# Attention and MoE on one core: the last batch's attention moved behind the start of the first pair, the sums of w_in moved to step 38, and a planner that prices VectorE and GpSimd meeting on a port

## The chip, the cores and the metric

One core of one Trainium2 chip runs the whole program. The metric is device time in microseconds; three runs of the kernel before took 879.83, 882.25 and 883.19 us, median 882.25. Engines are named as in the profile: PE is TensorE, DVE is VectorE, ACT is ScalarE, POOL is GpSimd, and SP is the queue from which nearly all DMAs are issued.

## The reference

Eight batches of softmax attention in its linear form (keys' softmax over the sequence, queries' over the head's 64 columns) feed a feed-forward block with a squared ReLU. All is float32.

```python
q_s = softmax(q, axis=-1); k_s = softmax(k, axis=2)      # 8 batches, 8 heads, 576 rows, 64 columns
kv = np.einsum('bhsd,bhse->bhde', k_s, v)
attn_out = np.einsum('bhsd,bhde->bhse', q_s, kv)
x = attn_out.transpose(0, 2, 1, 3).reshape(B * S, H * D)  # 4608 x 512
r = np.maximum(x @ w_in, 0.0)                             # w_in 512 x 2048
out = (s * (r * r) + b) @ w_out                           # w_out 2048 x 512
```

## The kernel before

**Blocks and steps.** Each batch gives one block of 512 rows; the 64 rows left over of each batch together form a ninth block. The 2048 inner columns are cut into 16 chunks. Blocks 0 to 4 run as 80 steps (`step(t)`, block t // 16, chunk t % 16): 12 matmuls make `h` for a chunk, ACT and DVE turn it into `r` and then into a high and a low float32r half (`gh`, `gl`; L1148, L1161, L1163, L1165), and 12 matmuls add it into the block's outputs (`acc`). Each product of two float32 numbers is three matmuls of such halves.

**Pairs.** Blocks 5 and 6, and then 7 and 8, run as pairs. For a pair, the first layer is done by a seven-product scheme instead of eight: `product` (L918) multiplies sums of quarters of w_in (names A11, S1 to S4 in `PROD`, stored in DRAM as `aset`, brought back through a ring of eight buffers by `ring_loads`) by sums of quarters of the two blocks (`B..`, `T..`), which lie as halves in the old weight slots (`b_cast`, `b_sums`, `stage_loads`). The sums of w_in's quarters are made on POOL by `a_sums`: 16 jobs of seven POOL instructions (L801, L804, four of L808, L812), one cast on ACT and two stores each. `quadrant` turns the products of one of eight rounds into four chunks; two of them go on at once, two are spilt to DRAM and come back later.

**Attention.** The attention of batches 2 to 7 goes on beside the steps. A batch has two `pr` (8 to 15 here are called pr 4 to 15, two per batch), each with two head pairs `u` (8 to 31). For a `pr`, `k_late` finds the keys' column maxima on DVE, sends them through DRAM (`k_out` L533, `k_in` L537), subtracts them and `k_exps` takes the exponential; `q_late` does the queries with two POOL instructions (L597, L614), and sends the turned halves through DRAM (L627, L634); `kv_late` and `x_late` make the matmuls on PE and evict them. Batches 3 and 4 write their result to DRAM and `x_back` brings it back in 512 KB pieces (L761), which ACT and DVE split into halves (L764, L766). In the kernel before all of it, but for the end of the last batch, stands ahead of the first pair.

**What sets the order.** `Order.run` is a planner that runs while the program is built. Every piece of work is a stream of `Op`s with an engine, a cost, a due time, needs (names of other ops' results, with a margin `late`) and buffers taken and freed; the planner takes the op that can start first (within NEAR the one due first), so that each engine's queue has a fixed order. At run time each engine then takes its queue in that order and an instruction waits for its data; everything behind it on that engine or queue waits too. The needs and costs exist in the planner alone: they change the order, not what an instruction waits for.

## Time and profile before

| what | value |
|---|---|
| median of three runs | 882.25 us |
| profiled execution | 883.05 us |
| its span, first to last instruction | 881.3 us |
| mean granted PE clock | 0.993 |
| PE busy | 844.0 us, 96% |
| DVE busy | 591.6 us, 67% |
| ACT busy | 440.2 us, 50% |
| POOL busy | 201.1 us, 23% |

The profiled execution lies 0.8 us above the median, and 1.75 us of it lie around its span. Busy shares are means over stages that differ: steps up to about 547 us, the first pair from there, the second pair from about 708 us. A wait is written with the engine that ended it; a line's idle time is that of its engine just before it.

### The profile page before, as it was taken

How to read it: one execution, taken by the hardware profiler on the slowest of the kernel's cores; microseconds unless marked ns; L12 is line 12 of the kernel's file. 1: busy time of each engine (PE TensorE's matmuls, PEld its weight loads, DVE VectorE, ACT ScalarE, POOL GpSimd, SP SyncE). 2: the span in 40 equal slices, each digit the busy share in tenths (PEclk: the TensorE clock that was granted, in tenths of full speed). 3: DMA queues.
4: the chain of work that ended last, by engine and by line, in shares of the span. 5: the costliest groups of instructions: out<-in, count | busy, mean ns of one | idle time of the engine just before them, and what ended most of it. 6: DMA issues, size and time to landing. Idle time of an engine off the chain costs nothing.

```text
span 881.3 us, 12571 instructions
## 1 busy us (share of the span) xinstructions
PE 844.0 (96%) x4358; PEld 690.6 (78%) x4358; DVE 591.6 (67%) x940; ACT 440.2 (50%) x720; POOL 201.1 (23%) x233
## 2 busy tenths in 40 slices
PE   7999999988999889987999999999999999999998
PEld 6788887877777668776788878888888888888886
DVE  6999977989987787867889764544457234434430
ACT  5998644644453454534455766533346243333430
POOL 1000035745662462435322232000013000000000
PEclk9999999999999999998999999999999999999999
DMA  9999157776679666767887734885554346555421
GB/s 274 322 387 304 58 150 204 200 189 160 185 184 241 172 178 183 204 183 193 201 232 182 184 101 118 276 265 153 165 152 161 85 143 193 157 161 159 167 73 48
DMA packets 175828, 161.82 MB, mean 184 GB/s; under 512 B 56468, under 2 KB 143508, under 8 KB 175764
## 3 DMA queue, kind: packets, MB, share of 16 engines
q1 hardware_dynamic: 174612, 159.89, 64.4%
q10 hardware_dynamic: 1152, 1.11, 0.4%
q8 instruction: 35, 0.57, 0.3%
q14 instruction: 29, 0.24, 0.1%
HBM read 106.43 MB, written 54.54 MB: 183 GB/s over the span
## 4 chain that ended last, share of the span: by engine, by line
PE 65%; DVE 16%; DMA 8%; issue 4%; ACT 3%; POOL 2%; SPq 1%; ACTq 0%; DVEq 0%; POOLq 0%
PE acc L1186 27%; PE h L1123 12%; PE bankU L932 10%; PE bankV L932 7%; PE last L1102 5%; DVE r L1161 2%; DMA back<-xs 2%; DVE gl L1165 2%; DMA area<-in_q_dram 2%; DVE y L722 2%; DMA turned<-area 1%; DVE area L623 1%; PE kv L314 1%; DVE area L618 1%; DVE kvf L672 1%
## 5 line engine op out<-in xcount | busy, mean ns | idle before, releaser
L1186 PE MATMUL acc<-w,gh 128*128 128x512 f32 x1024 | 319.5, 393 | 0.0
L1123 PE MATMUL h<-x,w 128*128 128x512 f32 x960 | 238.3, 395 | 9.8 <-ACT r L1148 9.7
L1186 PEld LDWEIGHTS acc<-w,gh 128*128 128x128 f32 x1024 | 190.3, 188 | 38.8 <-ACT o L1203 0.4
L1123 PEld LDWEIGHTS h<-x,w 128*128 128x128 f32 x960 | 180.4, 190 | 49.8 <-ACT r L1148 11.7
L1186 PE MATMUL acc<-w,gl 128*128 128x512 f32 x512 | 201.6, 394 | 4.7 <-DVE gl L1165 4.6
L1186 PEld LDWEIGHTS acc<-w,gl 128*128 128x128 f32 x512 | 96.4, 188 | 28.8 <-DVE gl L1165 8.4
L932 PE MATMUL bankU<-w,ring 128*128 128x512 f32 x378 | 96.0, 390 | 0.0
L1148 ACT ACTIVATE r<-h 128x512 f32<-128x512 f32 x80 | 47.7, 596 | 75.0 <-PE h L1123 64.1
L932 PEld LDWEIGHTS bankU<-w,ring 128*128 128x128 f32 x378 | 70.9, 188 | 14.6
L1009 DVE TENSOR_TENSOR rows<-bankV,rows 128x512 f32<-128x512 f32 x48 | 33.2, 691 | 61.1 <-PE bankV L932 31.4
L1163 ACT ACTIVATE gh<-r,sb 128x512 fp32r<-128x512 f32 x69 | 49.8, 722 | 44.3 <-DVE r L1161 43.8
L932 PE MATMUL bankV<-w,ring 128*128 128x512 f32 x282 | 71.6, 389 | 0.0
L1017 DVE SCALAR_TENSOR_TENSOR rows<-rows,sb 128x512 f32<-128x512 f32 x64 | 49.2, 772 | 32.6 <-ACT rows L1011 23.5
L1165 DVE SCALAR_TENSOR_TENSOR gl<-r,sb,gh 128x512 fp32r<-128x512 f32 x69 | 62.7, 909 | 7.1 <-ACT gh L1163 6.3
L1161 DVE SCALAR_TENSOR_TENSOR r<-r,sb 128x512 f32<-128x512 f32 x69 | 57.7, 836 | 14.6 <-ACT r L1148 14.4
L932 PEld LDWEIGHTS bankV<-w,ring 128*128 128x128 f32 x282 | 53.0, 188 | 11.0
L597 POOL TENSOR_TENSOR area<-area,qm 128x640 f32<-128x640 f32 x24 | 32.9, 1372 | 88.4 <-DVE qm L595 76.1
L904 POOL TENSOR_TENSOR stage<-stage 128x1024 f32<-128x1024 f32 x8 | 21.4, 2675 | 138.4 <-DVE w L889 138.1
L1011 ACT ACTIVATE rows<-rows 128x512 f32<-128x512 f32 x48 | 30.1, 627 | 43.9 <-DVE rows L1009 43.9
L1007 ACT COPY rows<-bankU 128x512 f32<-128x512 f32 x48 | 28.2, 588 | 47.2 <-PE bankU L932 47.1
L1029 DVE SCALAR_TENSOR_TENSOR gl<-rows,sb,gh 128x512 fp32r<-128x512 f32 x32 | 24.0, 751 | 35.8 <-ACT gh L1027 35.7
L614 POOL TENSOR_TENSOR qe<-qe,qr 128x640 f32<-128x640 f32 x24 | 33.5, 1396 | 43.7 <-DVE qr L610 16.0
(159 smaller groups left out, 1056.1 us busy)
## 6 DMA issues: line engine op xcount, KB each, us to landing
ring<-aset SPq DMA_DIRECT2D x110, 256.0 KB, 2.9
spare<-turned SPq DMA_DIRECT2D x48, 320.0 KB, 6.0
st<-in_moe_w_in_dram SPq DMA_DIRECT2D x16, 512.0 KB, 7.6
st<-in_moe_w_out_dram SPq DMA_DIRECT2D x16, 512.0 KB, 8.4
out_dram<-o SPq DMA_DIRECT2D x16, 512.0 KB, 3.1
aset<-S SPq DMA_DIRECT2D x32, 256.0 KB, 3.4
spilt<-rows SPq DMA_DIRECT2D x32, 256.0 KB, 3.1
turned<-qe SPq DMA_DIRECT2D x24, 320.0 KB, 3.5
```

The source lines that it names most:

```text
L597: nc.gpsimd.tensor_tensor(out=qt, in0=qt, in1=bc(qm, [P, 2, NT, D]), op=ALU.subtract)
L614: nc.gpsimd.tensor_tensor(out=qe_, in0=qe_, in1=qr, op=ALU.mult)
L932: nc.tensor.matmul(out_, w[:, a, c * P:(c + 1) * P], slot(k, c)[:, b_], start=k in (0, 1, 3) and n == 0, stop=n == 5, skip_group_check=True)
L1009: nc.vector.tensor_tensor(out=row(), in0=BANK["V"], in1=row(), op=ALU.add)
L1017: nc.vector.scalar_tensor_tensor(out=r, in0=r, scalar=s_col, in1=r, op0=ALU.mult, op1=ALU.mult)
L1102: nc.tensor.matmul(banks[j], g[:, js], w_, start=(f == 0 and n == 0), stop=(f == NFC - 1 and n == 2))
L1123: nc.tensor.matmul(hp_, w[:, j, c, :], x[:, c, :], start=(c == 0 and i == 0), stop=(c == NP - 1 and i == 2))
L1148: nc.scalar.activation(r, hp_, AF.Relu)
L1161: nc.vector.scalar_tensor_tensor(out=r, in0=r, scalar=s_col, in1=r, op0=ALU.mult, op1=ALU.mult)
L1163: nc.scalar.activation(gh, r, AF.Identity, bias=b_col)
L1165: nc.vector.scalar_tensor_tensor(out=gl, in0=r, scalar=b_col, in1=gh.bitcast(F32), op0=ALU.add, op1=ALU.subtract)
L1186: nc.tensor.matmul(acc[blk, j // 2][:, j % 2], g[:, js], w_, start=(f == 0 and i == 0), stop=(f == NFC - 1 and i == 2))
```

## The change

The planner's `Op` gets a kind "DVEp" for DVE instructions that read two tensors from SBUF: where POOL is planned busy at their start, 0.65 of the meeting is added to their cost. `k_fold` is priced 0.7 instead of 0.5. `WAIT`, the margin ahead of attention's matmuls, goes from 1.5 to 2.5. `a_sums` may not be planned before the step of its due time, and these run from step 38 at 2.4 steps each instead of from 18 at 3.5. The last batch's loads (pr 14 and 15) need step 72's h in the plan, and the pair's first products no longer need the end of that batch's keys and queries: the first six rounds keep their rows in the places of `stage_0` whose sums are already cast, and only rounds 6 and 7 use the old place of the queries (`rows`). In return the second pair's stage, which shares the buffer, is loaded after those rows are gone. pr 13 no longer has the second key buffer (`kalt`).

```diff
         def __init__(self, eng, cost, due, needs=(), take=(), free=(), gives=(), kb=0, late=0.0):
-            self.eng, self.cost, self.due, self.kb, self.late = eng, cost, due, kb, late
+            self.port = eng == "DVEp"
+            self.eng, self.cost, self.due, self.kb, self.late = eng[:3] if self.port else eng, cost, due, kb, late
...
+        SHARE = 0.65
...
-                heads[i][1] = end = self.at[eng] = t + o.cost * (2 if eng == "PE" and t < self.COLD else 1)
+                shared = min(o.cost, max(0.0, self.at.get("POOL", 0.0) - t)) * self.SHARE if o.port else 0.0
+                heads[i][1] = end = self.at[eng] = t + o.cost * (2 if eng == "PE" and t < self.COLD else 1) + shared
...
-        yield Op("DVE", 0.5, due)
+        yield Op("DVE", 0.7, due)
         k_fold(top)
...
-        yield Op("POOL", 0.85, due, needs=["mid"] + ([f"S {p} 0"] if c else [f"S {p - 1} 1"] if p else []), take=["tmp", "soft", "slow"])
+        yield Op("POOL", 0.85, due, needs=["mid", f"h{int(due)}"] + ([f"S {p} 0"] if c else [f"S {p - 1} 1"] if p else []), take=["tmp", "soft", "slow"])
...
-            before = [] if n else ([f"h{(FIRST - 1) * NFC - 1}"] if i == 0 else [f"T{i - 1} {m} {c}" for m in range(NPROD) for c in range(2)])
+            before = [] if n else ([f"h{(FIRST - 1) * NFC - 1}"] if i == 0 else 
+                [f"spilt{PAIRS[0][1] * NFC + 2 * NSTAGED - k}" for k in (1, 2)] + [f"g{PAIRS[0][0] * NFC + 2 * NSTAGED - k}" for k in (1, 2)]
+                + [f"T{i - 1} {m} {c}" for m in range(NPROD) for c in range(2)]
+            )
...
-        due = tau(i) - 8 + 0.3 * m
+        due = tau(i) - (8 if i == 0 else 1) + 0.3 * m
...
-            yield Op("DVE", 0.75, due, gives=[f"T{i} {m} {c}"])
+            yield Op("DVEp", 0.75, due, gives=[f"T{i} {m} {c}"])
...
-    ROWS = {"u1": 2, "u2": 2, "u3": 2, "u4": 1}
+    ROWS = {"u1": (2, "T3"), "u2": (2, "T2"), "u3": (2, "T1"), "u4": (1, "T4")}
...
+    NSTAGED = 6
...
+        n, name = ROWS[hold]
+        k = used[hold] % n
+        used[hold] += 1
+        if i == 0 and p < NSTAGED:
+            return staged(i, name)[:, k]
...
-        ready = [f"kv{2 * B - 1}", f"q{4 * B - 1} turned"] * (i == 0 and p == 0)
+        x = [x for _, x, _ in PROD].index(ROWS[hold][1])
+        ready = [f"T{i} {x} {c}" for c in range(2)] if i == 0 and p == 0 else [f"kv{2 * B - 1}", f"q{4 * B - 1} turned"] * (i == 0 and p == NSTAGED)
...
-    DUE_S, PACE_S = 18, 3.5
-    WAIT = 1.5
+    DUE_S, PACE_S = 38, 2.4
+    WAIT = 2.5
...
-        return NP < pr < 2 * FIRST + 4 and pr % 2
+        return NP < pr < 2 * FIRST + 2 and pr % 2
...
-        there = [f"w{NFC - 1} 1 there"] if pr == NP else []
+        there = [f"w{NFC - 1} 1 there"] if pr == NP else [f"h{FIRST * NFC - 8}"] if paired(pr // 2) else []
```

The same kind "DVEp" is given, with costs unchanged, to `k_max_2`, `k_max_0`, `k_under`, the queries' low half, `x_back`'s low half, the rows' squares, and the `r` and `gl` of most steps.

What the change makes of POOL's queue, where the queries of the second batch (`qe_10` to `qe_11`, lines L614 before and L617 after) stand among the sums (`S_p_c`). First before:

```order
L597 TENSOR_TENSOR area_87<-area_87,qm_10_1634 128x640
L681 TENSOR_TENSOR spare_1387<-kvf_83,spare_1387 128x2x128
L597 TENSOR_TENSOR area_87<-area_87,qm_11_1676 128x640
L614 TENSOR_TENSOR qe_10_1656<-qe_10_1656,qr_10_1684 128x640
L801 TENSOR_TENSOR S_1_0_1727<-w_2_505 128x2x128
L804 TENSOR_TENSOR S_1_0_1727<-w_3_574 128x2x128
L614 TENSOR_TENSOR qe_11_1702<-qe_11_1702,qr_11_1733 128x640
```

And the same stretch after, where L600 and L617 are the queries' two lines, L684 the keys' and values' product, and L589 a clearing of padding:

```order
L600 TENSOR_TENSOR area_87<-area_87,qm_10_1589 128x640
L617 TENSOR_TENSOR qe_10_1619<-qe_10_1619,qr_10_1648 128x640
L684 TENSOR_TENSOR spare_1381<-kvf_83,spare_1381 128x2x128
L600 TENSOR_TENSOR area_87<-area_87,qm_11_1656 128x640
L589 MEMSET kalt_1384 64x2x64 x2
L617 TENSOR_TENSOR qe_11_1692<-qe_11_1692,qr_11_1726 128x640
```

No sum stands among them any more; the first one (`S_0_0`) now follows the subtraction for `u` 18.

On the SP queue, what stands ahead of the second reload of block 4 (`back_4_1`, issued by L761 before). Before:

```order
L627 DMA turned_22_3749<-qe_22_3502 128x2x320
L627 DMA turned_22_3749<-area_87 128x2x320
L533 DMA maxima_13_3801<-sb_85 32x4x2
L634 DMA spare_1387<-turned_21_3514 64x8x160 x2
L290 DMA area_87<-in_q_dram 128x2x256
L291 DMA area_87<-in_q_dram 64x2x64
L815 DMA aset_6_109<-S_6_1_3730 128x4x128 x2
L752 DMA xs_5_100<-y_20_3780 128x576
L537 DMA misc_90<-maxima_13_3801 128x256
L627 DMA turned_23_3866<-qe_23_3702 128x2x320
L627 DMA turned_23_3866<-area_87 128x2x320
L761 DMA back_4_1_3893<-xs_4_99 128x2x512
```

After, on the same queue, with L764 as the reload:

```order
L303 DMA area_87<-in_v_dram 128x4x64 x4
L304 DMA area_87<-in_v_dram 64x4x64
L844 DMA ahead_3656<-aset_0_103 128x512 x2
L293 DMA area_87<-in_q_dram 128x2x256
L294 DMA area_87<-in_q_dram 64x2x64
L637 DMA spare_1381<-turned_22_3610 64x8x160 x2
L818 DMA aset_2_105<-S_2_0_3639 128x4x128 x2
L755 DMA xs_5_100<-y_21_3676 128x576
L630 DMA turned_23_3759<-qe_23_3637 128x2x320
L630 DMA turned_23_3759<-area_87 128x2x320
L764 DMA back_4_1_3778<-xs_4_99 128x2x512
```

The maxima of pr 13 (`maxima_13`) have left this place and stand 14 rows behind the reload; a store of sums is still ahead of it, and so are the turned queries of `u` 23.

On PE, in the first round of the first pair, after the change (L938 is `product`, L1199 the outputs, L699 attention's narrow products):

```order
L938 MATMUL bankU_5099<-w_4_654,ring_5079 128x512 x3
L938 MATMUL bankU_5099<-w_5_679,ring_5079 128x512 x3
L938 MATMUL bankV_5116<-w_6_704,ring_5079 128x512 x3
L938 MATMUL bankV_5116<-w_7_757,ring_5079 128x512 x3
L699 MATMUL xp_28_0_5171<-spare_1381 128x320 x2
L938 MATMUL bankU_5099<-w_8_814,ring_5079 128x512 x3
L938 MATMUL bankU_5099<-w_9_798,ring_5079 128x512 x3
```

Before, `xp_28_0` stood just ahead of step 72 and only the two products of `u` 31 lay in this round. Now those of `u` 28 to 31 lie in rounds 0 to 5, and the keys' and values' product of pr 15 in round 3.

## Rows read from the trace of the kernel before

**Rows 1.** the page: TensorE's busy us, share of the span, instructions

```profile
...
PE 844.0 (96%) x4358; PEld 690.6 (78%) x4358; DVE 591.6 (67%) x940; ACT 440.2 (50%) x720; POOL 201.1 (23%) x233
...
```

**Rows 2.** windows: us; busy us of PE, PEld, DVE, ACT, POOL; clock; DMA; GB/s

```profile
...
40.00:120.00 80.00, 80.00 (x433) 65.74 (x432) 73.85 (x102) 64.46 (x88) 1.05 (x6) 1.00 0.75 252
120.00:276.00 156.00, 148.70 (x823) 119.95 (x823) 140.71 (x241) 74.31 (x130) 85.50 (x99) 1.00 0.70 181
276.00:420.00 144.00, 126.81 (x712) 101.84 (x711) 108.77 (x194) 65.08 (x110) 62.59 (x73) 0.96 0.74 193
420.00:547.00 127.00, 125.23 (x630) 103.12 (x629) 94.46 (x156) 76.98 (x136) 36.92 (x31) 1.00 0.64 164
547.00:635.00 88.00, 88.00 (x391) 72.98 (x390) 39.79 (x57) 36.49 (x60) 0.00 (x0) 1.00 0.72 219
...
```

**Rows 3.** TensorE's waits from 120 to 276 us: total us, times, longest us

```profile
...
PE acc L1186 <- DVE gl L1165: 2.4, 4, 1.4
...
```

**Rows 4.** TensorE's waits from 276 to 420 us

```profile
...
PE h L1123 <- ACT r L1148: 8.8, 3, 7.3
PE xq L739 <- DVE kvf L672: 4.2, 3, 2.4
...
PE kv L314 <- DVE y L722: 1.7, 1, 1.7
...
```

**Rows 5.** groups on VectorE, 40 to 120 us: busy us, mean ns | idle

```profile
...
L1165 DVE SCALAR_TENSOR_TENSOR gl<-r,sb,gh 128x512 fp32r<-128x512 f32 x13 | 9.5, 729 | 0.1
L1161 DVE SCALAR_TENSOR_TENSOR r<-r,sb 128x512 f32<-128x512 f32 x12 | 8.9, 739 | 2.2 <-ACT r L1148 2.2
...
```

**Rows 6.** groups on VectorE, 120 to 276 us

```profile
...
L1161 DVE SCALAR_TENSOR_TENSOR r<-r,sb 128x512 f32<-128x512 f32 x24 | 23.7, 987 | 1.8 <-ACT r L1148 1.6
L1165 DVE SCALAR_TENSOR_TENSOR gl<-r,sb,gh 128x512 fp32r<-128x512 f32 x24 | 21.6, 901 | 2.4 <-ACT gh L1163 2.2
L623 DVE TENSOR_TENSOR area<-area,qe 128x640 f32<-128x640 f32 x10 | 11.6, 1165 | 0.6 <-ACT qe L621 0.4
L618 DVE STREAM_TRANSPOSE area<-qe 128x640 f32<-128x640 f32 x10 | 8.3, 832 | 1.8 <-POOL qe L614 1.8
...
L722 DVE TENSOR_TENSOR y<-xp,y 64x320 f32<-64x320 f32 x14 | 6.8, 485 | 0.3
...
```

**Rows 7.** groups on GpSimd, 120 to 276 us

```profile
...
L808 POOL TENSOR_TENSOR S<-S 128x128 f32<-128x128 f32 x36 | 21.9, 610 | 2.3
...
L812 POOL TENSOR_TENSOR S<-S 128x512 f32<-128x512 f32 x9 | 13.1, 1458 | 7.6 <-ACT S L810 6.8 <-DMA area<-in_q_dram 0.7
L801 POOL TENSOR_TENSOR S<-w 128x256 f32<-128x256 f32 x10 | 10.2, 1022 | 12.4 <-DMA aset<-S 8.3 <-DMA out_dram<-o 3.9
L804 POOL TENSOR_TENSOR S<-w 128x256 f32<-128x256 f32 x9 | 8.0, 888 | 0.1
...
```

**Rows 8.** timeline of 374.5 to 377 us: start, us, engine, line

```profile
...
374.68 1.53 POOL L614 TENSOR_TENSOR qe<-qe,qr 128x640 f32<-128x640 f32 x1 [2.33 <-issue]
...
375.01 1.75 DVE L1165 SCALAR_TENSOR_TENSOR gl<-r,sb,gh 128x512 fp32r<-128x512 f32 x1
...
```

**Rows 9.** line 764, ScalarE's casts of the reloaded blocks: what ended its idle time

```profile
...
  DMA back<-xs: 26.1, 4
...
```

**Rows 10.** timeline of the SP queue, 374 to 406 us

```profile
...
382.07 0.33 SPq L533 DMA_DIRECT2D maxima<-sb  x1
...
393.02 1.10 SPq L761 DMA_DIRECT2D back<-xs  x1
...
```

**Rows 11.** timeline of ScalarE, 374 to 406 us

```profile
...
400.00 1.04 ACT L764 CAST x<-back 128x1024 fp32r<-128x1024 f32 x1 [12.16 <-DMA back<-xs]
...
```

**Rows 12.** timeline of GpSimd, 505 to 549 us, and what ended its idle time

```profile
...
537.38 5.20 POOL L904 TENSOR_TENSOR stage<-stage 128x1024 f32<-128x1024 f32 x2 [12.37 <-DVE w L889]
```

**Rows 13.** timeline of TensorE, 546 to 556 us

```profile
...
550.02 1.52 PE L932 MATMUL bankU<-w,ring 128*128 128x512 f32 x6
...
```

**Rows 14.** the page, DMA issues: KB each, median us to landing

```profile
...
ring<-aset SPq DMA_DIRECT2D x110, 256.0 KB, 2.9
...
```

More of the change, by code (lines that the diff above doesn't have):

```diff
@@ L556, in k_late @@
         due = begin(pr)
-        yield Op("DVE", 0.69, due, needs=[f"ks{pr} there"], take=["m2", "m1"], late=SLACK)
+        yield Op("DVEp", 0.69, due, needs=[f"ks{pr} there"], take=["m2", "m1"], late=SLACK)
         kt = by_head(tiles[pr][0])
@@ L560, in k_late @@
         k_max_2(kt, m2)
-        yield Op("DVE", 0.85, due)
+        yield Op("DVEp", 0.85, due)
         k_max_0(kt, m2, m1)
@@ L574, in k_late @@
             yield Op(
-                "DVE", 0.82, due, needs=[f"mb{pr}"] * (1 - i), late=SLACK * (1 - i), free=["mb"] if i else (), gives=[f"k{2 * pr + i} less"]
+                "DVEp", 0.82, due, needs=[f"mb{pr}"] * (1 - i), late=SLACK * (1 - i), free=["mb"] if i else (), gives=[f"k{2 * pr + i} less"]
             )
@@ L764, in x_back @@
         nc.scalar.copy(xh, t)
-        yield Op("DVE", 1.25, due, free=["tmp", "soft", "slow"], gives=[f"x{u}" for u in us])
+        yield Op("DVEp", 1.25, due, free=["tmp", "soft", "slow"], gives=[f"x{u}" for u in us])
         nc.vector.tensor_tensor(out=xl, in0=t, in1=xh.bitcast(F32), op=ALU.subtract)
@@ L1001, in row @@
             if not cell:
-                cell.append(next_row(hold))
+                cell.append(next_row(i, p, hold))
             return cell[0]
@@ L1012, in quadrant @@
         else:
-            yield Op("ACT", 0.55, due - 1, needs=[f"P5 {i} {p}"], take=[hold], gives=[f"c21 {i} {p}"], late=LAG)
+            yield Op("ACT", 0.55, due - 1, needs=[f"P5 {i} {p}"] + ready, take=[hold], gives=[f"c21 {i} {p}"], late=LAG)
             nc.scalar.activation(row(), BANK["U"], AF.Relu)
         r = row()
-        yield Op("DVE", 0.8, due + away)
+        yield Op("DVEp", 0.8, due + away)
         nc.vector.scalar_tensor_tensor(out=r, in0=r, scalar=s_col, in1=r, op0=ALU.mult, op1=ALU.mult)
@@ L1027, in quadrant @@
         nc.scalar.activation(gh, r, AF.Identity, bias=b_col)
-        yield Op("DVE", 0.8, due, free=[hold], gives=[f"g{t}"])
+        yield Op("DVEp", 0.8, due, free=[hold], gives=[f"g{t}"])
         nc.vector.scalar_tensor_tensor(out=gl, in0=r, scalar=b_col, in1=gh.bitcast(F32), op0=ALU.add, op1=ALU.subtract)
@@ L1065, in make @@
             nc.scalar.activation(gh, r, AF.Identity, bias=b_col)
-            yield Op("DVE", 0.8, due, free=[where(f)], gives=[f"g{t}"])
+            yield Op("DVEp", 0.8, due, free=[where(f)], gives=[f"g{t}"])
             nc.vector.scalar_tensor_tensor(out=gl, in0=r, scalar=b_col, in1=gh.bitcast(F32), op0=ALU.add, op1=ALU.subtract)
@@ L1163, in step @@
             nc.scalar.activation(gh, r, AF.Identity, bias=b_col)
-            yield Op("DVE", 0.66, t - 2, free=["r"], gives=[f"g{t}"])
+            yield Op("DVEp", 0.66, t - 2, free=["r"], gives=[f"g{t}"])
             nc.vector.scalar_tensor_tensor(
@@ L1344, in attention_moe @@
         "acc": 2, "big": 1, "sm": 1, "h": 1, "r": 1, "g": 2, "ke": 1, "qf": 1, "qe": 2, "m2": 1, "m1": 1, "top": 1,
-        "maxima": 2, "turned": 2, "tmp": NTMP, "soft": NTMP - 1, "slow": 1, "mb": 1, "w": NFC + 1, **ROWS, "ring": NRING, "land": NLAND
+        "maxima": 2, "turned": 2, "tmp": NTMP, "soft": NTMP - 1, "slow": 1, "mb": 1, "w": NFC + 1, **{k: n for k, (n, _) in ROWS.items()}, "ring": NRING, "land": NLAND
     }, idle)
```

14 lines of the change are left out of this document (7 added, 7 removed).

## The prediction

> **What bounds the kernel now.** I read the page first: PE is busy for 844.0 of 881.3 us [rows 1], so whatever an order can win lies in PE's remaining 37 us, the first stretch of which is the start-up that the change leaves alone. The second view is the busy time by stretch [rows 2]. From 547 us PE is busy for 88.00 of 88 us: nothing can be won there. From 40 to 120 us likewise 80.00 of 80. The losses lie between 120 and 420 us: 156 - 148.70 = 7.3 us before 276 us, and 144 - 126.81 = 17.2 us from there to 420. From 420 to 547 it is 127 - 125.23 = 1.8 us. In the second of these stretches the granted clock is 0.96 on the mean: of its two levels, 2.4 and 1.2 GHz, the lower one must have held for 2 x 0.04 x 144 = 11.5 us, after PE had waited; in that time half the work was done, which is up to 5.8 us more. All that there is to win is thus 7.3 + 17.2 + 5.8 + 1.8 = 32.1 us.
>
> The third view says who ends those waits. Up to 276 us it is DVE, `gl` above all with 2.4 us in four waits [rows 3], and there DVE is busy for 140.71 of 156 us, 90%, with POOL busy for 85.50 beside it [rows 2]. From 276 to 420 us the largest is h waiting for ACT's `r`: 8.8 us in three waits, 7.3 in one; then kvf and y on DVE with 4.2 and 1.7 [rows 4]. The 7.3 us were not ACT's work. ACT stood idle for 12.16 us at the head of its queue before the cast of a reloaded block [rows 11], which that block's steps needed only some nine steps later. Its four casts of this kind cost ACT 26.1 us of idling [rows 9]. The reload itself was issued at 393.02, and the SP queue had last been held at 382.07 until DVE had folded the keys' maxima [rows 10]. So the pattern is one: DVE runs late against the plan, a queue that holds its order passes the lateness on, and PE stops.
>
> **What the change does, part by part.**
>
> *The sums before step 38.* In 120 to 276 us, POOL spends 21.9 + 13.1 + 10.2 + 8.0 = 53.2 us on nine of the sixteen sums [rows 7], 62% of its 85.5. DVE pays for POOL's company: `r` takes 739 ns and `gl` 729 where POOL is all but idle [rows 5], and 987 and 901 here [rows 6]. On 24 of each that is 24 x 0.248 + 24 x 0.172 = 10.1 us; at the sums' share of POOL, 62%, some 6.3 us come back on these two lines alone, and DVE's idle time goes from 15 to over 21 us. ACT loses nine casts too. PE can get at most its 7.3 us here. At the other end it gets nothing, if DVE's own chain of the attention sets the waits whoever is beside it. I take 5, nearer the upper end, since the waits are short and behind `gl`, the very instruction that was stretched. The sums now begin in the second stretch: step 55 began at about 400 us [rows 11] and the pair stands in step 80's place at 547, and 17 steps of 6 to 7 us back from 400 lie step 38 and 280 to 300 us.
>
> *The sums after step 38, and the last batch.* The second stretch held about six sums and will hold about as many; they come to lie beside the same attention. What pays for those that come on top later is the last batch: it leaves the steps. Of its DVE work four forms alone are 4 units x (1165 + 832 + 2 x 485) ns = 11.9 us [rows 6] (the second half of y left out); the maxima, reductions, and kvf come on top, and I put the whole at 30 us, an estimate at two and a half times these forms. It goes into the first pair, where from 547 to 635 us DVE is busy for 39.79 of 88 us and POOL for none [rows 2]. Its work on PE moves with it and costs the same there. The end of the steps, 420 to 547 us, has 1.8 us to win; I take 1.
>
> *The planner's prices.* One meeting shows the size: POOL's 1.53 us at 374.68 and a `gl` that starts at 375.01 and takes 1.75 us instead of 0.73 [rows 5, 8], 1.02 us more; the plan before gave it nothing. The new plan adds 0.65 of what is left of POOL's work, 0.65 x 1.20 = 0.78 us. `k_fold` at 0.7 for four small instructions, and 1 us more of margin before attention's matmuls cost nothing in themselves: they put PE's own steps ahead in its queue, which has work there (80 steps of 24 matmuls). For the second stretch this is what counts, with the reload. On the SP queue the hold by the maxima of pr 13 no longer stands ahead of `back_4_1`; a store of sums and the turned queries of `u` 23 do. On ACT the cast still stands behind `gh` of step 54, so the same wait can return. The stretch can give back all its 17.2 + 5.8 = 23.0 us, or nothing, or take a few more. I take 12, about half: of kvf and y, 5.9 us [rows 4], the better part, and of the large wait and the clock's 5.8 us something over half.
>
> *The first pair.* Three things are added. First, its second pair of differences on POOL, which waited 12.37 us for casts and ran at 537.38 [rows 12], now stands behind a sum's seven instructions and a clearing of the last batch's key padding, which waits for that batch's maxima. PE wants its cast at 550.02 [rows 13]. From 537.38 + 2.6 for the first difference and about 3 for its casts that leaves some 7 us of cover; costed at nothing, and one for one beyond. Second, instructions of the last batch stand between the rounds on DVE and ACT, where PE passes from one product to the next with little spare. I take 2 us for both, between 0 and 20. Third, DMA: by the sizes in the code about 4.9 MB of the last batch's traffic fall after the pair's start (four stores and six loads of 320 KB, v, and four results). From 420 to 547 us a share of 0.64 moved 164 GB/s [rows 2], 256 at a full share; 4.9 MB are 19 us. Idle in 547 to 635 us are 0.28 x 88 = 24.6 us, and the second stage's load leaves it. A ring load lands in 2.9 us [rows 14] and eight are held, so I cost this at nothing; it has little to spare.
>
> *The second stage loaded later.* Between the pairs stand the outputs of 14 steps, 14 x 12 matmuls at 88.00 / 391 = 0.225 us [rows 2], 38 us, ahead of the first product that needs it. That covers it: nothing.
>
> Sum: 5 + 1 + 12 - 2 = 16 us. From 883.05, the profiled execution, that gives 867.0; it lies 0.8 above the median, so **866 us** for the median.
>
> **A rule weighed.** The Trainium skill's "SBUF — State Buffer", section "SBUF: two separate sides", says that a DVE instruction with two SBUF inputs and a GpSimd instruction that reads SBUF shut each other out for the whole instruction: the later one waits to the end. By that rule the `gl` above would take 1.20 + 0.73 = 1.93 us; it took 1.75, so the trace comes to 0.85 of a full lock in this meeting. A plan at 0.65 is then still short, which speaks for the first rival.
>
> **Rivals.**
>
> *The reload still waits.* The casts stay in ACT's queue, a meeting costs 1.02 us where the plan now has 0.78, and POOL's sums lie beside the reloads of block 4. Then DVE is late again after 276 us, ACT stands at the cast, and the stretch gives back only 4 of 23 us: 883.05 - 0.8 - (5 + 1 + 4 - 2) = 874 us. For it: all four casts found ACT idle before [rows 9], not just one. Against: the maxima's hold is gone from the queue ahead.
>
> *All of it goes.* With DVE's load lower in the first stretch the attention is ahead by some steps when the second begins: x of `u` 19 stands at step 48 in PE's queue instead of 51. Then most of 32 us goes and the pair costs 1: 882.25 - 31 = 851 us. For it: the waits have one cause. Against: an order with no wait at all in 300 us of mixed work is rare.
>
> *Slower: the first pair waits.* One mechanism: the last batch's DMA-fed instructions (maxima, turned queries) stand at the heads of ACT's and DVE's queues between the rounds, and the rounds' evictions stand behind them. Each of `u` 28 to 31 and the maxima of pr 15 can hold a queue once by 4 or 5 us, about what the large waits of [rows 4, 9] were worth each, past the slack of one product. Five holds are 23 us; with a gain of 18 elsewhere that is 882.25 + 5 = 887 us. It decides once the holds sum to more than 18 us. For it: from 547 us nothing waits today, so any hold there is loss. Against: 3 us of margin are planned before every such instruction, and DVE is more than half idle.
>
> *Waits change place.* The new order removes these waits and its own take their place in the steps: 880 to 884 us, taken as 882.
>
> **How the numbers follow.** The forecast, 858 to 872 us, gets 0.50; all of it goes, 848 to 858, 0.16; the reload still waits, 872 to 879, 0.17; waits change place, 0.07; slower, 0.10. The range for 8 in 10 is 848 to 882: it leaves out the slower rival, the edge of waits that change place, and what a full gain with a free pair would give. Half a percent, 4.4 us, is about what a measurement of this kernel can tell from no change. Faster by more, below 877.8: 0.50 + 0.16 and most of 0.17, 0.79. Within: 0.10. Slower: 0.11.
>
> **What would show it.** In the profile after: no L804 to L815 on POOL before about 270 us, `r` and `gl` near 0.8 us in 120 to 276 us and PE idle there under 3 us; PE's wait for ACT's `r` in 276 to 420 us at 4 us or less, and the granted clock there at 0.98 or more; PE still busy in the first pair, with attention's narrow products between the rounds and no wait over 2 us. I am wrong if ACT's wait for the reload stays at 20 us or more in all, if PE waits at the first pair's start, or if the ring's loads land late.

## The result, and the profile after

Four runs of the changed kernel took 866.98 to 870.10 us, median 867.68; four of the kernel before 879.83 to 883.19, median 882.33. The ratio is 0.9843, with an interval of 0.9815 to 0.9872. The forecast was 866 us, 848 to 882. The profiled execution is the longest of the four (870.1 us, span 868.2), so its rows show 13.1 us of the gain, and not the median's 14.7.

The busy times by stretch of the changed kernel, to hold against [rows 2] (columns: the stretch, its length, busy time and count of PE, its weight loads, DVE, ACT and POOL, the granted clock, DMA share, GB/s):

```profile
120.00:276.00 156.00, 153.59 (x849) 126.20 (x848) 133.12 (x247) 75.28 (x129) 38.24 (x43) 0.99 0.67 166
276.00:420.00 144.00, 137.92 (x739) 112.66 (x738) 119.18 (x204) 70.83 (x123) 67.15 (x79) 0.98 0.76 200
420.00:547.00 127.00, 121.02 (x600) 98.48 (x599) 89.33 (x124) 71.90 (x119) 74.35 (x77) 1.00 0.61 170
527.60:651.00 123.40, 121.22 (x571) 99.44 (x570) 78.36 (x125) 59.09 (x103) 22.00 (x21) 1.00 0.82 243
```

The last row is the first pair, which now begins at 527.6 us. The same pair before:

```profile
547.00:664.00 117.00, 117.00 (x519) 97.00 (x518) 55.13 (x78) 49.33 (x81) 5.33 (x2) 1.00 0.68 203
```

PE's busy time rises by 153.59 - 148.70 = 4.9 us in the first stretch and by 137.92 - 126.81 = 11.1 in the second. The granted clock goes from 0.96 to 0.98 in the second and from 1.00 to 0.99 in the first; over the whole span it is 0.993 in both kernels. In the third, PE was idle for 1.8 us before and is for 6.0 now: 3.8 in the steps up to 527.6 us and 2.2 in the pair. The pair takes 6.4 us longer: 121.22 - 117.00 = 4.2 are PE work with 52 more matmuls, the last batch's, which only changed places; the other 2.2 us are that idle time, all of it before 547 us.

PE's waits in the second stretch, to hold against [rows 4], and below them those from the pair's start to the end of the first pair (columns: what waited, for whom, us in all, times, the longest):

```profile
PE h L1136 <- ACT r L1161: 3.0, 2, 2.8
PE acc L1199 <- DVE gl L1178: 1.5, 1, 1.5
PE xq L742 <- DVE kvf L675: 0.8, 1, 0.8
PE kv L317 <- issue: 0.7, 1, 0.7
...
PE acc L1199 <- DVE gl L1171: 1.4, 1, 1.4
PE acc L1199 <- ACT gh L1169: 0.6, 1, 0.6
PE bankV L938 <- DVE stage L1022: 0.2, 1, 0.2
```

The 8.8 us for `r` are 3.0, but another 1.9 us now lie in the first stretch, where they were 0.5. How the two large ones came about stands on ACT and PE (columns: start, us, engine, line, operation, and in brackets the idle time before it and who ended it):

```profile
255.28 1.05 ACT L767 CAST x<-back 128x1024 fp32r<-128x1024 f32 x1 [4.08 <-DMA back<-xs]
...
259.06 3.46 PE L1136 MATMUL h<-x,w 128*128 128x512 f32 x8 [1.88 <-ACT r L1161]
...
285.36 0.75 ACT L719 COPY y<-xq 64x256 f32<-64x256 f32 x2
292.16 1.04 ACT L767 CAST x<-back 128x1024 fp32r<-128x1024 f32 x1 [6.05 <-DMA back<-xs]
293.11 0.59 ACT L1161 ACTIVATE r<-h 128x512 f32<-128x512 f32 x1
...
293.75 1.65 PE L1136 MATMUL h<-x,w 128*128 128x512 f32 x3 [2.79 <-ACT r L1161]
```

It is the pattern of [rows 9, 11] again: ACT stands for 4.08 and for 6.05 us at the cast of a reloaded block, `r` is queued behind it, and PE loses 1.9 and 2.8 us. The four casts still cost ACT 16.0 us of idling, after 26.1. And after both waits the lower of the two clock levels is granted (the columns are those of [rows 2]; the two stretches are those in which the clock was low):

```profile
259.50:262.90 3.40, 3.40 (x10) 2.66 (x9) 3.27 (x7) 1.35 (x2) 0.20 (x1) 0.50 0.22 87
293.60:300.40 6.80, 5.94 (x48) 4.66 (x49) 6.06 (x13) 1.95 (x4) 2.06 (x2) 0.50 0.57 171
```

Before, it was low in these:

```profile
316.80:320.30 3.50, 3.50 (x10) 2.73 (x9) 3.22 (x6) 3.28 (x8) 3.50 (x3) 0.51 0.51 151
398.80:405.60 6.80, 4.01 (x9) 3.15 (x10) 4.53 (x5) 4.88 (x9) 1.83 (x2) 0.50 0.72 184
```

That is about 10.2 us in either kernel: the clock as a whole gave nothing back.

On DVE in the first stretch, `r` and `gl` (count, busy us, mean ns, idle before), to hold against [rows 6]:

```profile
L1174 DVE SCALAR_TENSOR_TENSOR r<-r,sb 128x512 f32<-128x512 f32 x25 | 21.4, 855 | 11.8 <-ACT r L1161 11.6
L1178 DVE SCALAR_TENSOR_TENSOR gl<-r,sb,gh 128x512 fp32r<-128x512 f32 x25 | 20.4, 816 | 2.4 <-ACT gh L1176 2.1
```

They fell from 987 and 901 ns, and the first sum on POOL starts at 270.52 us. So the signs that the prediction named are there, though a part of the wait and of the low clock has only moved into the first stretch. Whether it is so for the reasons forecast, the profile alone can't say.

### The profile page after: what moved, and what is told of

It is laid out like the page before. It is cut to its first block, busy times and chain, and to the rows that moved or that the text cites. A ratio compares the mean times of both kernels' runs of the same rounds, so it can differ in the third digit from the quotient of the medians.

```text
span 868.2 us, 12561 instructions
## 1 busy us (share of the span) xinstructions
PE 842.8 (97%) x4358; PEld 691.7 (80%) x4358; DVE 593.9 (68%) x940; ACT 439.7 (51%) x720; POOL 197.9 (23%) x233
## 4 chain that ended last, share of the span: by engine, by line
PE 75%; DMA 8%; DVE 6%; issue 4%; POOL 3%; SPq 3%; ACT 1%; ACTq 0%; POOLq 0%; DVEq 0%
PE acc L1199 31%; PE h L1136 17%; PE bankU L938 9%; PE bankV L938 7%; PE last L1115 5%; PE kv L317 2%; DMA back<-xs 2%; DMA aset<-S 1%; DMA area<-in_v_dram 1%; POOL S L811 1%; DMA xs<-y 1%; POOL S L815 1%; DMA spare<-turned 1%; DMA turned<-area 1%; DMA area<-in_q_dram 1%
## 5 line engine op out<-in xcount | busy, mean ns | idle before, releaser
L1199 PE MATMUL acc<-w,gh 128*128 128x512 f32 x1024 | 317.8, 391 | 0.6 <-ACT gh L1169 0.6
L1199 PEld LDWEIGHTS acc<-w,gh 128*128 128x128 f32 x1024 | 190.3, 188 | 39.9 <-ACT gh L1169 1.0
L1199 PE MATMUL acc<-w,gl 128*128 128x512 f32 x512 | 200.4, 391 | 6.8 <-DVE gl L1171 5.2
L1199 PEld LDWEIGHTS acc<-w,gl 128*128 128x128 f32 x512 | 96.1, 188 | 29.8 <-DVE gl L1171 6.7
L938 PE MATMUL bankU<-w,ring 128*128 128x512 f32 x378 | 96.1, 389 | 0.0
L938 PEld LDWEIGHTS bankU<-w,ring 128*128 128x128 f32 x378 | 70.7, 188 | 14.6 <-ACT stage L1020 0.2
L1174 DVE SCALAR_TENSOR_TENSOR r<-r,sb 128x512 f32<-128x512 f32 x69 | 60.1, 871 | 29.8 <-ACT r L1161 29.4
L938 PE MATMUL bankV<-w,ring 128*128 128x512 f32 x282 | 71.7, 390 | 0.2 <-DVE stage L1022 0.2
L938 PEld LDWEIGHTS bankV<-w,ring 128*128 128x128 f32 x282 | 52.9, 188 | 11.6 <-DVE stage L1022 0.6
L1178 DVE SCALAR_TENSOR_TENSOR gl<-r,sb,gh 128x512 fp32r<-128x512 f32 x69 | 55.6, 805 | 6.4 <-ACT gh L1176 5.6
L600 POOL TENSOR_TENSOR area<-area,qm 128x640 f32<-128x640 f32 x24 | 33.9, 1413 | 82.8 <-DVE qm L598 82.4
L1022 DVE TENSOR_TENSOR rows<-bankV,rows 128x512 f32<-128x512 f32 x30 | 20.7, 691 | 39.4 <-ACT rows L1020 19.4
L1030 DVE SCALAR_TENSOR_TENSOR rows<-rows,sb 128x512 f32<-128x512 f32 x40 | 31.3, 785 | 20.7 <-ACT rows L1024 14.9
L617 POOL TENSOR_TENSOR qe<-qe,qr 128x640 f32<-128x640 f32 x24 | 33.0, 1377 | 54.0 <-issue 23.4
L811 POOL TENSOR_TENSOR S<-S 128x128 f32<-128x128 f32 x64 | 39.1, 612 | 4.5
L1115 PE MATMUL last<-w,w 128*128 128x512 f32 x168 | 38.2, 389 | 0.0
L1115 PEld LDWEIGHTS last<-w,w 128*128 128x128 f32 x168 | 31.5, 188 | 6.5
```

The lines of the kernel that those rows point to most:

```text
L600: nc.gpsimd.tensor_tensor(out=qt, in0=qt, in1=bc(qm, [P, 2, NT, D]), op=ALU.subtract)
L617: nc.gpsimd.tensor_tensor(out=qe_, in0=qe_, in1=qr, op=ALU.mult)
L811: nc.gpsimd.tensor_tensor(out=o, in0=x, in1=y, op=op)
L938: nc.tensor.matmul(out_, w[:, a, c * P:(c + 1) * P], slot(k, c)[:, b_], start=k in (0, 1, 3) and n == 0, stop=n == 5, skip_group_check=True)
L1030: nc.vector.scalar_tensor_tensor(out=r, in0=r, scalar=s_col, in1=r, op0=ALU.mult, op1=ALU.mult)
L1115: nc.tensor.matmul(banks[j], g[:, js], w_, start=(f == 0 and n == 0), stop=(f == NFC - 1 and n == 2))
```

## The experiments

In two tables, since the kernels are compared with each other. The first gives the ratio to the kernel before on the same chip, with its interval, and the idle time of ACT at the four casts of reloaded blocks. Below it stands how much earlier or later than in the kernel before a step begins (the start of ACT's `r` of that step, in the profiled execution), and the span's end.

```
kernel      made from  edit                              median  ratio [95%]              casts' idle
b_sums      before     sums from step 38                 883.91  0.9992 [0.9974, 1.0009]  17.2
b_prices    before     all prices                        872.39  0.9862 [0.9837, 0.9886]  18.9
b_share     before     the meeting's price alone         871.24  0.9856 [0.9829, 0.9883]  12.5
b_batch     before     last batch moved alone            876.76  0.9926 [0.9904, 0.9947]  20.0
a_nosums    after      sums back at step 18              872.69  0.9895 [0.9867, 0.9922]  14.3
a_noprice   after      no prices                         877.29  0.9924 [0.9899, 0.9948]  15.7
a_share1    after      meeting priced in full            867.49  0.9815 [0.9785, 0.9845]  15.5
b_mem       before     sums' POOL work as clearings      872.67  0.9863 [0.9837, 0.9889]  28.7
b_land      before     cast needs the landing            896.07  1.0154 [1.0122, 1.0186]   0.0
a_land      after      cast needs the landing            857.55  0.9723 [0.9695, 0.9750]   0.9
a_land6     after      the same, 6 us of margin          856.04  0.9704 [0.9677, 0.9731]   0.0
f_land      after      the same, sums due before use     864.36  0.9778 [0.9751, 0.9804]   0.0

step             28     36     40     48     56     76    end
before        211.5  262.3  289.8  347.1  406.5  527.6  881.3
after          -4.3   -3.9   -7.3   -7.1  -17.2  -20.3  -13.1
b_sums         -4.8   -2.1   +1.4   -2.8   -0.9   +0.4   +0.8
b_prices       -2.8   -4.0   -6.2   -7.3  -11.4  -11.4  -11.4
b_share        -3.8   -6.1   -5.1   -6.6  -13.1  -11.9  -12.0
b_batch        +0.7   +0.6   +1.5   +1.0   -7.8  -11.0   -6.2
a_nosums       -3.4   -4.6   -6.9   -9.0  -16.8  -17.1  -10.9
a_noprice      -4.2   -1.8   +0.1   -4.1   -4.8  -12.7   -6.3
b_mem          -5.0   -7.2   -5.4   -8.3   -9.2   -9.9  -10.0
b_land         +0.8   +1.0   +0.4  +21.1  +12.3  +11.4  +10.2
a_land         -3.8   -7.3  -10.9  -17.1  -28.0  -35.2  -25.9
f_land         -4.1   -6.9   -9.7   -5.4  -15.9  -23.7  -19.0
```

Where the last batch is moved, about 4 us of what step 76 shows is PE's work that now lies in the pair, and it is missing again at the end.

### Which of the three parts pays

**The sums alone.**

```diff
-needs=["mid"] + ([f"S {p} 0"] if c ...
+needs=["mid", f"h{int(due)}"] + ([f"S {p} 0"] if c ...
-    DUE_S, PACE_S = 18, 3.5
+    DUE_S, PACE_S = 38, 2.4
```

> The kernel before with one part of the change: the sums of w_in from step 38 on at 2.4 steps each, the planner's prices and the last batch as before. If the sums' company on GpSimd makes VectorE late in 120 to 276 us, the waits of TensorE there (7.3 us) go as in the full change, `r` and `gl` fall to about 0.8 us there, and the time is 876 to 879 us (ratio 0.993 to 0.996); the later stretch, which now holds all sums beside the last batch, may give 2 to 5 us of it back. If the gain hangs on the plan's prices or on the room that the last batch leaves, the time is 882 us or more (ratio 1.00 to 1.01).

The ratio is 0.9992: nothing, as the second case of the expectation has it. Its first two stretches:

```profile
120.00:276.00 156.00, 150.53 (x831) 122.73 (x830) 133.18 (x248) 74.72 (x127) 37.45 (x37) 0.99 0.65 167
276.00:420.00 144.00, 129.54 (x683) 104.32 (x682) 115.08 (x198) 65.24 (x112) 74.20 (x83) 0.95 0.71 186
```

POOL falls from 85.50 to 37.45 us and DVE from 140.71 to 133.18, as the prediction had it, and step 28 begins 4.8 us earlier. Up to there the sums' move does what was forecast: PE waits for `gl` no more, and its busy time, first before and then here, is

```profile
120.00:212.00 92.00, 86.91 (x477) 70.32 (x478) 82.91 (x138) 44.76 (x79) 50.32 (x57) 1.00 0.70 180
120.00:212.00 92.00, 90.00 (x504) 74.01 (x503) 81.69 (x147) 44.68 (x76) 21.52 (x23) 1.00 0.61 152
```

But the lead is gone by step 40 (+1.4 us). In the new order a reload's cast stands in this stretch, where before the first one ran at 284.04, and ACT idles there:

```profile
252.97 1.05 ACT L764 CAST x<-back 128x1024 fp32r<-128x1024 f32 x1 [4.19 <-DMA back<-xs]
254.57 1.65 PE L1123 MATMUL h<-x,w 128*128 128x512 f32 x6 [1.22 <-ACT r L1148]
```

The lower clock is granted for 3.4 us from 267.4 us, and from 276 to 300 us PE waits for 2.1 us for `r` and for 2.0 us for a product on POOL (`spare`, L681). Later the last cast holds ACT for 8.59 us. The room that DVE gains is time that PE gains only as far as the next such wait.

**The prices alone.**

```diff
+            self.port = eng == "DVEp"
...
+        SHARE = 0.65
...
+                shared = min(o.cost, max(0.0, self.at.get("POOL", 0.0) - t)) * self.SHARE if o.port else 0.0
-        yield Op("DVE", 0.5, due)
+        yield Op("DVE", 0.7, due)
-    WAIT = 1.5
+    WAIT = 2.5
```

The kind "DVEp" is given as in the change.

> The kernel before with the planner's part alone: two-input VectorE instructions priced by 0.65 of their meeting with GpSimd, the maxima's fold at 0.7, the margin before attention's matmuls at 2.5 us. If a plan that knows the meetings avoids the waits, the stretches 120 to 276 and 276 to 420 us lose about half of their 24.5 us of waiting: 870 us (ratio 0.986). If the work itself has to move, the waits only change place: 880 to 884 us (ratio 1.00). If the reloaded blocks' casts wait for their landing because the plan leaves the landing out, ScalarE's wait at those four casts stays at 20 us or more here.

0.9862, nearly the whole gain: its interval, 0.9837 to 0.9886, and that of the whole change overlap widely. Its first stretch, the two lines of DVE there, and PE's waits there:

```profile
120.00:276.00 156.00, 152.72 (x850) 125.17 (x849) 140.37 (x242) 78.94 (x136) 85.28 (x97) 1.00 0.75 189
```

```profile
L1164 DVE SCALAR_TENSOR_TENSOR r<-r,sb 128x512 f32<-128x512 f32 x25 | 22.9, 915 | 2.8 <-ACT r L1151 2.5
L1168 DVE SCALAR_TENSOR_TENSOR gl<-r,sb,gh 128x512 fp32r<-128x512 f32 x25 | 22.8, 912 | 1.5 <-ACT gh L1166 1.4
```

```profile
PE xq L742 <- DVE kvf L675: 1.9, 2, 1.2
PE xp L742 <- DMA spare<-turned: 1.1, 1, 1.1
PE kv L317 <- DVE y L725: 0.3, 1, 0.3
```

This is the row to learn from. POOL is as busy as before (85.28 us), DVE too (140.37), `gl` is as slow (912 ns), and yet no wait for `gl` is left [rows 3] and PE is busy for 152.72 us instead of 148.70. The instructions take their time as before; the plan now knows it and puts other work of PE ahead of what will be late. In the second stretch PE is busy for 133.00 us, after 126.81, although it still waits for `r` for 8.6 us in three waits. The casts' idling, 18.9 us, lies just under the 20 of the expectation, so that sign decides nothing here.

**The meeting's price alone** leaves the two other prices of that edit as they were:

```diff
-        yield Op("DVE", 0.7, due)
+        yield Op("DVE", 0.5, due)
-    WAIT = 2.5
+    WAIT = 1.5
```

> The kernel before with the meetings priced at 0.65 and nothing else: the fold stays at 0.5, the margin before attention's matmuls at 1.5 us. With all three prices it was 0.9862. If the meeting is what the plan lacked, 0.984 to 0.990. If the margin did it, 0.993 or more, and TensorE's waits for kvf and y come back to 5 us or more between 120 and 420 us.

0.9856, as the first case has it: `SHARE` does it, and the margin and the fold's price add nothing that these runs can tell.

**The last batch alone** is the changed kernel with the sums and the prices undone:

```diff
-        SHARE = 0.65
+        SHARE = 0.0
-        yield Op("DVE", 0.7, due)
+        yield Op("DVE", 0.5, due)
-    DUE_S, PACE_S = 38, 2.4
-    WAIT = 2.5
+    DUE_S, PACE_S = 18, 3.5
+    WAIT = 1.5
```

> The changed kernel with prices and sums put back as before: only the last batch's attention lies behind the start of the first pair. If room in the steps is what counts, the steps end earlier by the last batch's own work on TensorE (about 5 us, which the first pair gets) and by some waits after step 64; nothing before step 54 changes by more than 1 us, and the large wait at step 55 stays: 879 to 884 us (ratio 0.996 to 1.002). If the last batch was what crowded the steps, 870 us or less (ratio under 0.987).

0.9926. Nothing moves before step 48; by step 56 it is 7.8 us ahead, so the large wait of [rows 4, 11] is gone without prices or sums: PE waits for `r` for 0.9 us in the second stretch. ACT's idling at the casts is still 20.0 us, 5.48 of it at the last cast, which was 12.16. The expectation was missed: the time lies between its two ranges, and the large wait, which was to stay, went.

**The whole change without the sums, and without the prices.**

```diff
-needs=["mid", f"h{int(due)}"] + ...
+needs=["mid"] + ...
-    DUE_S, PACE_S = 38, 2.4
+    DUE_S, PACE_S = 18, 3.5
```

> The changed kernel with the sums of w_in from step 18 at 3.5 steps each, as before: prices and last batch changed alone. The prices alone gave 0.9862 and the full change 0.9843. If the sums' place matters only with the room that the last batch leaves, this is 872 to 876 us (0.987 to 0.991); if prices and last batch do all of it, 866 to 870 us (0.982 to 0.986).

```diff
-        SHARE = 0.65
+        SHARE = 0.0
-        yield Op("DVE", 0.7, due)
+        yield Op("DVE", 0.5, due)
-    WAIT = 2.5
+    WAIT = 1.5
```

> The changed kernel without the planner's prices (no meeting priced, the fold at 0.5, the margin at 1.5 us): sums and last batch moved alone. The sums alone gave 0.9992, the last batch alone 0.9926. If the moves help each other, 870 to 874 us (0.985 to 0.990). If the prices are what makes either of any use, 877 us or more (0.993 and up), with VectorE's `gl` or kvf ending most of TensorE's waits between 276 and 420 us.

Without the sums' move 0.9895, without the prices 0.9924. Both times fit a case of their expectations, but the sign named for the second is not there: `gl` and kvf end 5.2 of PE's 12.0 us of waits between 276 and 420 us, less than half. From these, with prices and batch there, the sums' place is worth 0.9895 - 0.9843 = 0.0052, some 5 us, though the two intervals touch; without prices it is worth nothing (0.9926 with the batch alone, 0.9924 with batch and sums). And the batch, worth 0.0074 alone, shows no gain on top of the prices: 0.9895 with both, 0.9862 with the prices alone, and these intervals overlap too. The three parts do not add: 0.8, 13.8 and 7.4 thousandths by themselves make 22.0, together 15.7. Batch and prices both win between steps 48 and 56 (8.8 and 4.1 us by the table; the changed kernel 10.1), and what is lost there can be won only once. That this is why they do not add is argued from the table; the rest of the difference is not placed.

### Is it the meeting itself

`b_mem` keeps the order of the kernel before and takes the reading out of the sums on POOL: their instructions only write zeros. The sums of w_in are thus left out of the pairs' first layer.

```diff
-        nc.gpsimd.tensor_tensor(out=F[:, 0:4:3], in0=h, in1=l, op=ALU.add)
+        nc.gpsimd.memset(F[:, 0:4:3], 0.0)
...
-        nc.gpsimd.tensor_tensor(out=F, in0=F, in1=high, op=ALU.subtract)
+        nc.gpsimd.memset(F, 0.0)
```

> The kernel before, every instruction in its place, but the sums' seven GpSimd instructions of each job are clears of the same tiles: the sums of w_in are left out of the result. A clear reads nothing from SBUF. If it is the meeting of reads that stretches VectorE, `r` and `gl` in 120 to 276 us fall from 0.99 and 0.90 to 0.85 and 0.80 us or less (the queries' GpSimd instructions still meet them), TensorE's waits there fall from 7.3 to 4 us or less, and the time is 868 to 878 us. If VectorE is late by its own chain, waits and time stay within 3 us of the kernel before. The wait of 12 us at the cast of the reloaded block should shrink where the hold by VectorE made it, and keep at least 4 us where it is the landing.

Same order, 0.9863; the two lines in the first stretch:

```profile
L1161 DVE SCALAR_TENSOR_TENSOR r<-r,sb 128x512 f32<-128x512 f32 x25 | 21.8, 871 | 3.8 <-ACT r L1148 3.7
L1165 DVE SCALAR_TENSOR_TENSOR gl<-r,sb,gh 128x512 fp32r<-128x512 f32 x25 | 20.5, 819 | 2.7 <-ACT gh L1163 2.5
```

987 and 901 ns become 871 and 819, a little above the 0.85 and 0.80 us expected, and PE idles in that stretch for 4.3 us instead of 7.3. POOL's instructions also became shorter (49.31 us instead of 85.50 in this stretch), so the run takes away the meetings and some of POOL's time at once; the latter alone was not run. Either the meetings go, or the plan is told of them: both ways are worth 12 us. The casts' wait stays (28.7 us, 12.15 of it at the last) and with it 6.6 us of PE at the large one.

**The price in full.**

```diff
-        SHARE = 0.65
+        SHARE = 1.0
```

> The changed kernel with the meeting priced in full instead of at 0.65, as a full lock would have it. If 0.65 leaves VectorE late, TensorE's waits for it between 120 and 540 us (8 us) halve and the time is 861 to 865 us (0.976 to 0.980). If what is left hangs on the reload, which the plan prices no better, it stays at 866 to 871 us (0.982 to 0.987) and ScalarE idles 12 us or more at the four casts.

0.9815 against 0.9843, with intervals that overlap widely: 0.65 and 1.0 can't be told apart. The time and the casts' idling (15.5 us) are those of the second case. That a plan at 0.65 is still short, as the prediction weighed it, is not borne out: the full price does not take more away than these runs can tell.

### The wait for the reload

The prediction took ACT's wait at the cast for lateness that the SP queue passes on. The hold that it named is there before, between 374 and 406 us (columns as for PE's waits):

```profile
SPq L533 <- DVE sb L529: 7.4, 1, 7.4
```

With a like hold, 6.8 us, the last cast idles for 12.15 us in `b_mem`; in `b_batch` and the changed kernel, where the maxima hold nothing there, for 5.48 and 2.08. But ACT idles at the other casts too. The planner's code shows another cause that can be tried: the cast has a margin `late=SLACK`, but no needs to which it could apply. The plan takes the data for there as soon as the load is issued, in all kernels above. So the landing becomes a need:

```diff
-take=["tmp", "soft", "slow"], kb=512, late=SLACK)
+take=["tmp", "soft", "slow"], kb=512, late=SLACK, gives=[f"back{bb} {k}"])
-        yield Op("ACT", 1.04, due, late=SLACK)
+        yield Op("ACT", 1.04, due, needs=[f"back{bb} {k}"], late=SLACK)
```

On the kernel before:

> The kernel before with one dependence more in the plan: the cast of a reloaded block needs the reload's landing (with the 3 us of margin that the cast already had, but that no need ever used). Cast and reload get other places, nothing else is told to the planner. If the 26.1 us that ScalarE idled at the four casts come from the landing that the plan leaves out, they fall under 8 us, the wait of 7.3 us at step 55 and the half clock behind it go, and the time is 870 to 876 us (ratio 0.986 to 0.993). If VectorE's lateness and the hold on the SP queue made them, at least 15 us of idling stay and the time is within 3 us of before.

On the changed kernel, and there with a margin of 6.0 instead of `SLACK`:

> The changed kernel with the landing of the reload as a need of the cast. It idled 16.0 us at the four casts, and TensorE waited 4.9 us for ScalarE's `r` behind two of them, with 10.2 us at half clock. If the landing is the cause, the idling falls under 6 us and the time to 860 to 864 us (ratio to before 0.975 to 0.980). If another order brings other waits of the same size, 865 to 870 us (0.981 to 0.987).

> As the last, with 6 us of margin after the planned landing instead of 3; reloads landed in 4.6 to 8.2 us where the plan has about 4.5. Idling at the four casts under 2 us if the plan's queue is kept; 859 to 864 us if the landing is the cause, 865 to 870 us if waits only change place.

The casts' lines of the changed kernel, then of `b_land` and `a_land` (the last column is ACT's idle time before them):

```profile
L767 ACT CAST x<-back 128x1024 fp32r<-128x1024 f32 x4 | 4.2, 1049 | 16.0 <-DMA back<-xs 16.0
```

```profile
L764 ACT CAST x<-back 128x1024 fp32r<-128x1024 f32 x4 | 4.1, 1036 | 0.0
```

```profile
L767 ACT CAST x<-back 128x1024 fp32r<-128x1024 f32 x4 | 4.2, 1043 | 0.9 <-DMA back<-xs 0.9
```

The wait goes in each of them (0 to 0.9 us in the four kernels with the need, 12.5 to 28.7 in the ten without), so the missing need is its cause; 3.0 us of margin are enough. What that is worth depends on what the new order puts in its place. On the order before, where 870 to 876 us were expected, it costs 1.5%: PE's two largest waits in `b_land`'s second stretch, and ACT's instruction behind the first:

```profile
PE xp L739 <- DVE y L722: 13.7, 1, 13.7
PE h L1123 <- ACT x L764: 5.7, 1, 5.7
```

```profile
353.81 0.85 ACT L716 COPY y<-xp 64x320 f32<-64x320 f32 x2 [4.53 <-DMA out_dram<-o]
```

The eviction of attention's result takes a buffer of the same pool as the blocks' outputs and the reloads, and it had to wait until the store of a block's output was through; the step's h, planned behind the reload, then waited for the cast too. On the changed order the kernels with the same need are shorter by 10 us and more: 0.9723 and 0.9704 against 0.9843, both below the ranges expected. But in these two, sums that are planned late are taken from weight slots that hold other data by then (in `a_land` the last job reads its two slots at 552.1 and 560.5 us, and spilt rows are loaded into slots from 545.2), so a part of the pairs' first layer is made of other numbers; the work is the same in kind and amount, but its order is one that the whole reference does not allow.

In `f_land` the sums are due early enough and the casts into the weight slots need them:

```diff
-        return [f"h{(FIRST - 1) * NFC + 2 * m + c}"] if i == 0 else ...
+        return [f"h{(FIRST - 1) * NFC + 2 * m + c}", f"S {m} 0", f"S {m} 1"] if i == 0 else ...
-    DUE_S, PACE_S = 38, 2.4
+    DUE_S, PACE_S = 32, 2.2
```

The loads of the spilt rows need the last job's sums in the same way.

> The changed kernel with the reload's landing as a need of its cast, the sums as needs of what overwrites their weights (the last casts into the weight slots, the spilt rows that come back), and the sums from step 32 at 2.2 steps each so that they are done before that. If the landing is what the changed kernel still loses, the casts' idling is under 3 us, TensorE waits under 5 us in all between 120 and 420 us, and the time is 855 to 862 us (ratio to before 0.969 to 0.977). If the two kernels that left the sums' needs out were only fast because their late sums ran past the steps, this one is at 864 to 870 us.

864.36 us, 0.9778: of the versions that compute the whole reference the fastest here. Its interval lies below that of the changed kernel (0.9815 to 0.9872) and overlaps that of `a_share1`. The casts idle no more, but the time is above the range for the landing, at the edge of that for the late sums, and PE waits for some 11 us between 120 and 420 us where under 5 were expected. So how much of the 10 us of `a_land` is the landing's, and how much came of sums that ran past the steps, is not shown; and since `f_land` also moves the sums, its own 0.0065, some 6 us, is not the need's alone. It loses 4.3 us between steps 40 and 48, where the wait of `b_land` returns in small:

```profile
332.86 1.03 ACT L767 CAST x<-back 128x1024 fp32r<-128x1024 f32 x1
340.01 0.85 ACT L719 COPY y<-xp 64x320 f32<-64x320 f32 x2 [6.12 <-DMA out_dram<-o]
```

The cast finds its data; the eviction behind it finds no buffer, and PE's largest wait here, 5.6 us for `r`, follows.

## Why the prediction was right, and which step of it was not

**The time and the stretches.** 866 us were forecast and 867.68 measured. Term by term, as PE's idle time: 5 us for the first stretch, 4.9 measured; 12 for the second, 11.1 measured; 1 for the end of the steps, where 2.0 us of idle came on top instead (3.8 up to the pair's start, after 1.8); -2 for the pair, 2.2 us of idle. The measured terms make 4.9 + 11.1 - 2.0 - 2.2 = 11.8 us; forecast were 16. The span is shorter by 13.1 us: PE's busy time as a whole is 1.2 us less (842.8 us, after 844.0 [rows 1]), which is not placed. One part of the 12 us did not come: the clock. It was low for about 10.2 us before (the prediction made 11.5 of it, from a rounded 0.96) and is for 10.2 after, a third of it now in the first stretch.

**The step that failed: what the 5 us were for.** The prediction gave them to the sums before step 38, since these make DVE slow, and let the prices count in the second stretch only. Measured as PE's busy time in the first stretch, against 148.70 us before, the sums alone bring 1.8 us (`b_sums`, 150.53), sums and batch 2.2 (`a_noprice`, 150.90), the prices alone 4.0 (`b_prices`, 152.72), prices and batch with the sums where they were as much (`a_nosums`, 152.75), and all three 4.9 (153.59). So most of it comes with the prices, which the prediction called nothing in themselves, and for its cause the near hit of 5 on 4.9 is luck. What went wrong in the argument: a stretched `gl` was taken as time that PE loses, and its end as time that PE keeps. In the old order it is lost indeed, since `b_mem`, with a shorter `gl` in the same order, brings 3.0 us there; but `b_prices` shows that the order decides, for with `gl` as slow as ever no wait for it is left. And `b_sums` shows that the time is not kept: up to 212 us the move wins 3.1 us, and waits at a cast and behind POOL in the new order take it back. With prices and batch in place the sums' move gives some 5 us as well, but after 276 us: PE is busy for 134.15 us there in `a_nosums` and for 137.92 in the changed kernel.

**The large wait.** It went where it stood, and ACT's wait at the casts is 16.0 us, under the 20 at which the prediction was to be wrong; but 2.8 us at another cast and 1.9 at a third, in the first stretch, came in place of the 7.3. The reason was only half seen. The cast stands too early because the plan has no landing time for it, not because a maximum holds the SP queue; the hold, as far as the rows show, only made that one wait as long as it was. The rival *the reload still waits* thus had its mechanism right at all four casts, and missed that the stretch gives back its 11.1 us all the same. What the casts' 16.0 us are worth can't be read from PE's waits of 1.9 and 2.8 us, and is not shown by the runs either: with the need in the plan the kernel is some 6 us shorter in `f_land`, where the sums moved too, and over 10 in the two whose late sums read other data. The rival *all of it goes* (851 us) would have needed that need too; `a_land6`, one of these two, comes nearest with 856.04.

**The first pair.** The slower rival did not come. PE does wait at the pair's start, which the prediction had named as a sign of being wrong, but for 2.2 us in three waits, 1.4 at the longest, where it had costed 2; after 547 us it waits no more. The ring's loads land in 3.0 us, after 2.9 [rows 14], with a DMA share of 0.82. That DMA had little to spare was right and did no harm.

**The end of the steps.** Forecast +1, measured 2.0 us of idle more from 420 us to the pair's start, where 3.8 us are two waits for the form of `gl` in L1171. One of them follows the meeting at 496 us that is shown below.

**Still open.** Prices with sums but without the batch were not run. Every edit makes another order, and `b_land` shows that this alone can move the time by over 1%; so differences of 2 or 3 us between single kernels are not put down to an edit here, that between the changed kernel (0.9843) and the meeting's price alone (0.9856) among them. The need for the landing was not run on the changed order with the sums both left where they are and read in time.

## What to carry to other kernels

When an order is planned ahead, to tell the plan of a cost can be worth as much as to remove the cost: pricing the meeting of VectorE and GpSimd won 12 us without making one instruction faster, taking GpSimd's reads away in the same order won 12 as well, and moving GpSimd's sums to another place won nothing by itself. Look for each instruction that is first to touch a DMA's data whether the plan knows the landing, and expect that mending it moves the wait to the next scarce thing, here a buffer. Before an effect is credited to an edit of several parts, run each part alone and each left out: the parts did not add.
